# RWKV-7 recurrence and hardswish feed-forward on one core: r and a turned by VectorE, k and the state as half turns

## The chip, the cores and the metric

One core of a Trainium2 chip runs the whole program. The metric is the device time of one execution in microseconds, as the median of several runs. TensorE (PE) multiplies matrices and turns tiles by multiplying with an identity. VectorE (DVE), ScalarE (ACT) and GpSimd (POOL) do the elementwise work, and the DMA queues of SyncE (SP) and ScalarE issue the transfers. Each engine works through its own instructions in order.

## What is computed

```python
# r, k, v, w, a, b: (4, 8, 768, 40) f32
for t in range(S):
    y[:, :, t] = np.einsum('bhd,bhde->bhe', rt, state)
    Sa = np.einsum('bhde,bhe->bhd', state, at)
    state_decay = state * wt[:, :, None, :] - np.einsum('bhd,bhe->bhde', Sa, bt)
    state = state_decay + np.einsum('bhd,bhe->bhde', vt, kt)
x = y.transpose(0, 2, 1, 3).reshape(3072, 320)
h = x @ w_in                                   # (3072, 2048)
out = (h * np.clip(h + 3.0, 0.0, 6.0) / 6.0) @ w_out
```

## The kernel before

The sequence is cut into chunks of 64 steps. A **unit** is one chunk of two batch elements with all 8 heads; there are 24 units (NK), in groups of four (NU), and partitions hold 2 x 64 time steps. Inside a unit the recurrence becomes matrix products: decay products along the chunk (two scans on VectorE), scores between a, b, k, v and r, the inverse of a triangular matrix, and an update of the state.

Each unit has a part that doesn't need the state, **prepared ahead** (`prepare`), and its **own** part (`step`):

- `prepare`: W turns w and scans it (L549, L560 in gam); A and B turn a and b and multiply them by the decays (L593, L601); F multiplies a by b; K turns k (L474, L681); factor turns the decays and builds a tile of weighted k and b on GpSimd (L668); E multiplies k by a and masks the product (L521); EV multiplies E by v.
- `step`: RT and VT turn r and v (L484, copied out of PSUM by ScalarE at L839 and L872); S turns the state (L879, L884); R, C, U, UT, rS, H are products; y (L975) gives the output and the state's update together, which VectorE adds (L982, L987) and GpSimd scales (L983); move and move2 send the result to a tile `xt` by eight small DMAs on SP.

What has to be transposed is turned on TensorE in one of two forms. `turn_pairs` (and S, L879) turns four full 128x128 tiles into a bank tagged "one". `turn_halves` (L484) turns eight 64-row halves into a pair of banks. Before the change, w, k and the state go by the full form, and a, b, r, v by halves in later units (`halves`: from unit 4 in `step`, from unit 8 in `prepare`).

From about 200 us on, the order of work is written out by a loop over **blocks**, four to a unit (L1424). The stages of the own unit and of the unit prepared ahead for each block stand in OWN_STAGES and AHEAD_STAGES (L1338 to L1341); CLOSE_STAGES serves units 8 to 11, whose beginnings lie closer together. In a block, `together` (L1353) first lets TensorE do the block's products in the order PRODUCTS, then gives the other engines their work on the results in the order RESULTS. It counts PSUM banks (five at most), and the pairs of banks ("pair") are used in rotation, two of them. At FIRST_NARROW, if a feed-forward expansion is open, its 64-row matmuls are put in and its results follow (L1094 ScalarE, L1095 VectorE).

Between blocks, `feed` hands out pieces of feed-forward work: `expand` (h, L1079) into two banks and `contract` (o, L1120). An expansion can't begin until VectorE has read the one before (L1095). Every fourth unit VectorE also inverts four units' triangular matrices (L746, L752, some 60 small operations and three transposes of 128x1024 at L726, L755, L760), laid between the feed-forward pieces from block 2 of one unit to block 0 of the next but one. The products L781 and L804 ("third block") then follow in blocks 0 and 1 of two units.

Inputs are fetched one unit ahead by `fetch` on SP's queue: two DMAs for w, a, b and k, four for r and v.

## Time and profile before

Three runs took 794.69, 796.5 and 797.93 us; the median is 796.5. The profiled execution took 794.59 us with a span of 792.9 us.

| engine | busy us (share of span) | instructions |
|---|---|---|
| PE matmul | 727.6 (92%) | 14552 |
| PE weight load | 615.8 (78%) | 14552 |
| DVE | 496.8 (63%) | 986 |
| ACT | 307.1 (39%) | 648 |
| POOL | 161.5 (20%) | 296 |

The mean granted TensorE clock is 0.961 of full speed. A busy share is a mean over stages with different limits, so it is read by stretches. Of the time on TensorE, the two feed-forward products take most: h 251.2 us busy in 2304 matmuls and o 230.2 us in 768. Matmuls overlap in the pipeline, so what one costs TensorE is read from the chain of work in order of time (start, duration, what), where each piece ends when the next begins.

### The profile page before, as it was taken

To read this page: it belongs to the slowest core of one execution; us is meant where nothing else is said; L and a number is where in the kernel's file an instruction comes from. 1 tells how busy PE (TensorE), PEld (TensorE's weight loads), DVE (VectorE), ACT (ScalarE), POOL (GpSimd) and SP (SyncE) were. 2 spreads that over 40 slices of the span, in tenths; PEclk is the share of its full clock that TensorE was granted. 3 is DMA by queue.
4 is the path that set the end of the run, shared out by engine and by line. 5 is a ranking of instruction groups with operands and counts; after the bars stand their busy time and mean duration, and the time that the engine had idled before them with its cause. 6 is when DMAs were issued, how large, how long until landed. Compare 5 with 4: busy or idle time off the path is not lost.

```text
span 792.9 us, 32747 instructions
## 1 busy us (share of the span) xinstructions
PE 727.6 (92%) x14552; PEld 615.8 (78%) x14552; DVE 496.8 (63%) x986; ACT 307.1 (39%) x648; POOL 161.5 (20%) x296
## 2 busy tenths in 40 slices
PE   5735778999999999999999999999999999999997
PEld 4624667878778878888888888788888888888886
DVE  7898887689446699445898345888335982323210
ACT  2347663222553424443324453334443324412211
POOL 6403012421223203112303121303111201000000
PEclk9756898999999999999999999999999999999999
DMA  9683662420334321333323233223233101110100
GB/s 121 118 201 84 156 149 51 77 49 9 65 61 76 70 55 31 65 59 62 58 42 58 49 60 70 43 46 56 51 59 58 21 19 38 38 34 13 21 19 17
DMA packets 195004, 48.14 MB, mean 61 GB/s; under 512 B 178224, under 2 KB 193584, under 8 KB 194864
## 3 DMA queue, kind: packets, MB, share of 16 engines
q1 hardware_dynamic: 190560, 45.31, 30.9%
q8 instruction: 115, 1.88, 1.0%
q10 hardware_dynamic: 4304, 0.74, 0.7%
q14 instruction: 25, 0.20, 0.1%
HBM read 34.08 MB, written 3.93 MB: 48 GB/s over the span
## 4 chain that ended last, share of the span: by engine, by line
PE 76%; DVE 10%; issue 4%; DMA 3%; SPq 2%; ACT 2%; POOL 1%; DVEq 0%; POOLq 0%; ACTq 0%
PE h L1079 26%; PE o L1120 24%; PE pair L512 4%; PE pair L975 4%; PE one L474 2%; PE pair L484 2%; PE pair L893 2%; PE pair L861 2%; PE pair L695 1%; DVE wm L560 1%; DVE prods L549 1%; PE pair L929 1%; PE pair L913 1%; DVE prod L746 1%; DVE x L752 1%
## 5 line engine op out<-in xcount | busy, mean ns | idle before, releaser
L1079 PE MATMUL h<-xt,win 128*128 128x128 f32 (+1 forms) x2304 | 251.2, 283 | 4.9 <-DVE gt L1095 4.9
L1079 PEld LDWEIGHTS h<-xt,win 128*128 128x128 f32 (+1 forms) x2304 | 231.6, 193 | 23.0 <-issue 4.4
L1120 PE MATMUL o<-wout,gt 128*128 128x320 f32 x768 | 230.2, 443 | 0.0
L1120 PEld LDWEIGHTS o<-wout,gt 128*128 128x128 f32 x768 | 138.3, 190 | 50.7
L1094 ACT ACTIVATE gt<-h,three 128x512 f32<-128x512 f32 x96 | 63.1, 687 | 110.9 <-PE h L1079 110.5
L1095 DVE SCALAR_TENSOR_TENSOR gt<-gt,h 128x512 f32<-128x512 f32 x96 | 62.2, 683 | 67.2 <-ACT gt L1094 66.9
L746 DVE TENSOR_TENSOR prod<-x 128x30 f32<-128x30 f32 (+9 forms) x180 | 65.0, 361 | 9.0 <-POOL x L731 3.5
L525 DVE COPY_PREDICATED store<-mask,pair 128x512 f32<-128x512 int32 x40 | 29.0, 725 | 62.6 <-PE pair L512 62.5
L752 DVE TENSOR_TENSOR x<-x,prod 128x30 f32<-128x30 f32 (+9 forms) x180 | 64.4, 358 | 5.5
L668 POOL TENSOR_TENSOR KBt<-K,rgt 128x320 f32<-128x320 f32 x19 | 16.4, 865 | 204.5 <-ACT rgt L657 184.4
L983 POOL TENSOR_TENSOR yg<-ys,gam 128x512 f32<-128x512 f32 x20 | 25.5, 1273 | 147.5 <-DMA R<-in_r_dram 69.6
L982 DVE TENSOR_TENSOR ys<-pair,ys 128x512 f32<-128x512 f32 x20 | 13.8, 690 | 48.7 <-PE pair L975 43.5
L549 DVE TENSOR_TENSOR_SCAN prods<-wm,start 128x528 f32<-128x528 f32 x24 | 33.5, 1401 | 10.7 <-ACT wm L546 10.2
L839 ACT ACTIVATE RT<-pair 128x512 f32<-128x512 f32 x21 | 12.5, 597 | 59.1 <-PE pair L484 59.0
L975 PE MATMUL pair<-store,KBt 64*64 64x104 f32 x1280 | 33.1, 252 | 0.0
L560 DVE TENSOR_TENSOR_SCAN wm<-wm,start 128x528 f32<-128x528 f32 x24 | 31.1, 1297 | 0.8
L700 ACT ACTIVATE EV<-pair 64x320 f32<-64x320 f32 x44 | 18.9, 430 | 31.8 <-PE pair L695 30.4
L1138 ACT ACTIVATE ob<-o 128x320 f32<-128x320 f32 x22 | 9.6, 436 | 55.3 <-PE o L1120 34.6
L975 PEld LDWEIGHTS pair<-store,KBt 64*64 64x64 f32 x1280 | 29.1, 133 | 1.5
L814 ACT ACTIVATE tinv<-pair 32x256 f32<-32x256 f32 x48 | 18.0, 375 | 31.0 <-PE pair L804 30.4
L865 DVE TENSOR_TENSOR RR<-pair,EV 128x320 f32<-128x320 f32 x21 | 10.3, 489 | 23.7 <-PE pair L512 20.5
L897 ACT ACTIVATE store<-pair 128x320 f32<-128x320 f32 x24 | 10.5, 437 | 37.0 <-PE pair L913 33.6
(278 smaller groups left out, 1072.4 us busy)
## 6 DMA issues: line engine op xcount, KB each, us to landing
V<-in_v_dram SPq DMA_DIRECT2D x96, 40.0 KB
out_dram<-ob SPq DMA_DIRECT2D x47, 80.0 KB
R<-in_r_dram SPq DMA_DIRECT2D x92, 40.0 KB
B<-in_b_dram SPq DMA_DIRECT2D x42, 80.0 KB
store<-V SPq DMA_DIRECT2D x20, 160.0 KB
W<-in_w_dram SPq DMA_DIRECT2D x37, 80.0 KB
A<-in_a_dram SPq DMA_DIRECT2D x37, 80.0 KB
K<-in_k_dram SPq DMA_DIRECT2D x37, 80.0 KB
```

The costliest lines, as they stand in the source:

```text
L512: nc.tensor.matmul(out=o[i][half(q), n, :], lhsT=lhs[half(i, D), n ^ (2 * q * swap), half(q)], rhs=rhs[half(i, D), n ^ (2 * q * back), hal ...
L525: nc.vector.copy_predicated(out=x[:, :, 0:BL].rearrange("p (h i) t -> p i h t", i=2), mask=mask8, data=o[2])
L549: nc.vector.tensor_tensor_scan(out=prods[:].rearrange("p r m i -> p (r m i)"), data0=wm[:, 0:SCAN], data1=start[:], initial=0.0, op0=ALU.m ...
L560: nc.vector.tensor_tensor_scan(out=back, data0=back, data1=start[:], initial=0.0, op0=ALU.mult, op1=ALU.add)
L746: nc.vector.tensor_tensor(out=pv, in0=_ap(x[:], (i + 1) * L + i, [[L, n], [0, i]]), in1=_ap(x[:], i * L, [[0, n], [1, i]]), op=ALU.mult,)
L752: nc.vector.tensor_tensor(out=rest, in0=rest, in1=pv, op=ALU.add)
L975: nc.tensor.matmul(out=y[q][half(s), pr, :], lhsT=o[name][half(q), h * D:h * D + SLOT], rhs=m[name][half(q), x, :], start=(name == "K" and ...
L983: nc.gpsimd.tensor_tensor(out=yg[:], in0=m["ys"][:].rearrange("p r q t -> p r (q t)"), in1=o["G"][:], op=ALU.mult)
L1079: nc.tensor.matmul(out=hp[c][:, i, :], lhsT=lhsT, rhs=rhs, start=(begun[c] == 0), stop=(begun[c] == 3 * NQ - 1))
L1094: nc.scalar.activation(out=gt[:], in_=hp[c][:], func=AF.Relu, bias=three[:], scale=1.0)
L1095: nc.vector.scalar_tensor_tensor(out=gt[:], in0=gt[:], scalar=6.0, in1=hp[c][:], op0=ALU.min, op1=ALU.mult)
L1120: nc.tensor.matmul(out=op[:], lhsT=gts[c][:, n, :], rhs=wout[:, c * HJ + r * NQ + n, :], start=((split or r == 0) and c == 0 and n == 0), ...
```

## The change

Four things are changed together.

1. **r and a** of later units (r from unit 5, a from unit 8) are loaded by quarters of 32 partitions with two time steps on a partition side by side (`fetch_blocks`), and turned by VectorE's transpose of 32x32 blocks (`turn_blocks`). No TensorE turn, no PSUM and, for r, no ScalarE copy remain. The product of a with the decays, on VectorE before, is a GpSimd instruction on SBUF. A load of a is four DMAs in place of two, one of r eight in place of four; each brings 320 bytes to a run where it was 160.
2. **k and the state** are turned as eight half turns where they were four full ones (k from unit 8, the state from unit 4).
3. **Stages are moved.** K goes from block 2 to block 3, E from block 3 to block 0 of the next unit's time (AHEAD_STAGES). PRODUCTS is reordered, RT is no product any more (RT0 is the old form, for unit 4), and only W is left ahead of FIRST_NARROW.
4. **Smaller things.** The four larger moves into `xt` are issued by ScalarE's queue in place of SP's. The tiles of a and r grow from 512 to 672 columns, and the feed-forward tile `gt` has four buffers in place of five.

```diff
+    def blocked(name, i):
+        return i >= {"A": 2 * NU, "R": NU + 1}.get(name, NK)
+    def fetch_blocks(name, x, b, g, fresh):
+        t = homes[name]
+        for s in range(2):
+            for c in range(2):
+                rows = slice(s * SLOT + c * L, s * SLOT + c * L + L)
+                at = x.offset + (b * H + s) * T * D + g * BL * D
...
+                if fresh and c:
+                    nc.gpsimd.memset(t[rows, H * 2 * D:], 0.0)
+                first = (1 - c) * L
+                for k in range(2 if name == "R" else 1):
+                    n = 4 if name == "R" else 8
+                    y = bass.AP(tensor=x.tensor, offset=at + (s + k) * T * D if name == "R" else at,
+                                ap=[[2 * D, L], [(4 if name == "R" else 2) * T * D, n], [1, 2 * D]])
+                    nc.sync.dma_start(out=t[rows, first + k * H * D:first + k * H * D + n * 2 * D].rearrange(
+                        "p (n e) -> p n e", n=n), in_=y)
+        return t
+    def turn_blocks(to, t, name):
+        to = to[:].rearrange("p (j r) (q t c) -> p j q r c t", j=2, q=2, c=2)
+        x = t[:, L:L + 2 * H * D].rearrange("p (n c e) -> p n c e", c=2, e=D)[:, :, :, 0:L]
+        if name == "R":
+            x = x.rearrange("p (j q r) c e -> p j q r c e", j=2, q=2)
+            for j in range(2):
+                nc.vector.transpose(out=to[:, j], in_=x[:, j])
+            return
+        to = to.rearrange("p j q r c t -> p q (j r) c t")
+        nc.vector.transpose(out=to, in_=x.rearrange("p (q r) c e -> p q r c e", q=2))
@@ a_stage
+            if halves:
+                nc.vector.memset(_ap(o["wm"][:], 0, [[HB + 1, 2 * NB + 1]]), 0.0)
+                turn_blocks(at, o["AN"], "A")
+                nc.gpsimd.tensor_tensor(out=at[:], in0=at[:], in1=o["G"][:], op=ALU.mult)
@@ k_stage
-            x = turn_pairs(o["KN"])
+            x = turn_in(o["KN"], halves)
...
@@ s_RT
+            m["RT"] = turned("RT")
+            if blocked("R", i):
+                turn_blocks(m["RT"], o["RN"], "R")
+            else:
...
@@ s_S
-            sp = ps_any([P, 2, 2, P])
+            sp = ps_pair(4, SLOT) if halves else ps_any([P, 2, 2, P])
...
+                    if halves:
+                        for s in range(2):
+                            nc.tensor.transpose(out=sp[s][:, 2 * q + j, :], in_=x[half(s)],
+                                                identity=ident[half(s), half(s)])
@@ s_move
-                nc.sync.dma_start(out=dst, in_=src)
+                (nc.scalar if halves else nc.sync).dma_start(out=dst, in_=src)
@@ results
-                gt = ffn.tile([P, NQ, P], F32, name="gt", bufs=5)
+                gt = ffn.tile([P, NQ, P], F32, name="gt", bufs=4)
@@ the order
-    AHEAD_STAGES = [["W", "gam"], ["A", "B"], ["F", "K"], ["E", "factor"], [], [], [], ["EV"]]
+    AHEAD_STAGES = [["W", "gam"], ["A", "B"], ["F"], ["K", "factor"], ["E"], [], [], ["EV"]]
-    PRODUCTS = ["W", "S", "K", "RT", "VT", "A", "B", "factor",
-                "y", "EV", "R", "C", "U", "UT", "rS", "H", "E", "F"]
-    RESULTS = ["RT", "y", "W", "VT", "EV", "R", "S", "C", "A", "B", "move", "move2",
+    PRODUCTS = ["W", "S", "B", "K", "factor", "VT", "RT0", "E",
+                "y", "R", "C", "U", "UT", "rS", "H", "EV", "F"]
+    RESULTS = ["RT", "RT0", "y", "W", "VT", "EV", "R", "S", "C", "A", "B", "move", "move2",
                "U", "UT", "rS", "F", "K", "H", "E", "factor", "beside", "gam"]
-    TURNS = PRODUCTS[:3]
+    TURNS = ["W"]
...
+            first = [["RT" if blocked("R", i) else "RT0", "VT"]]
+            own[i, m] = step(i), first + OWN_STAGES[1:]
```

## The prediction

> **What bounds the kernel now.** I read the busy slices first (40 slices of 19.8 us), then busy time by stretches of 30 us, then the chain of waits in order of time, and last VectorE's and GpSimd's timelines inside one unit.
>
> ```profile
> PE   5735778999999999999999999999999999999997
> DVE  7898887689446699445898345888335982323210
> ...
> 440.00:470.00 30.00, 29.74 (x708) 25.56 (x701) 12.44 (x22) 15.82 (x38) 5.35 (x9) 1.00 0.34 61
> 470.00:500.00 30.00, 30.00 (x638) 25.63 (x637) 16.80 (x32) 11.57 (x27) 7.12 (x14) 1.00 0.34 59
> 500.00:530.00 30.00, 29.05 (x448) 24.60 (x448) 27.22 (x62) 9.24 (x21) 5.44 (x9) 1.00 0.27 48
> 710.00:740.00 30.00, 30.00 (x541) 25.87 (x540) 6.55 (x11) 7.70 (x15) 1.27 (x1) 1.00 0.15 32
> ```
>
> The columns of the stretches are length, then busy us of PE, PEld, DVE, ACT, POOL, then the granted clock, the DMA share and GB/s. From 200 us to the end PE is busy without a gap to speak of: 581.05 us of 593, where some 4 us are the wind-down behind the last matmul and 7.8 us are stalls. The granted clock there is 1.00, so no work is slowed by it. Whatever TensorE work is taken away after 200 us shortens the run, until another engine makes TensorE wait. The engine nearest to that is VectorE: 27.22 us of 30 in the stretch with an inversion (500 to 530), 12 to 17 in the others, and there alone PE loses nearly 1 us.
>
> **What TensorE loses.** Two pieces of the chain in order of time price the turns (start, us, what).
>
> ```profile
> 456.96 0.89 PE h L1079 x8
> 457.86 0.44 PE one L879 x4
> 458.29 1.09 PE h L1079 x16
> 459.38 0.49 PE pair L484 x16
> ```
>
> Four full turns of the state take 0.44 us, sixteen half turns 0.49, so eight take 0.245. Removed or shortened:
> - a, units 8 to 23: 16 x 0.245 = 3.9 us.
> - r, units 5 to 23: 19 x 0.245 = 4.65 us.
> - k, units 8 to 23, full to half: 16 x (0.44 - 0.245) = 3.1 us.
> - the state, units 4 to 23: 20 x 0.195 = 3.9 us.
>
> Together **15.6 us**, all behind 200 us; a steady unit loses 0.88 us of about 27. The switch from 128-row to 64-row matmuls (0.16 to 0.2 us: L484 x16 takes 0.65 directly behind o or full turns) stays once per block. Bank counts, worked out by `together`'s rule, stay within five in every steady block (5, 4, 4, 4 where it was 5, 5, 5, 4), so no block is split anew.
>
> **What the other engines gain, and what hides it.** The transposes come from this row, the GpSimd product from the next:
>
> ```profile
> L760 DVE STREAM_TRANSPOSE tt<-x 128x1024 f32<-128x1024 f32 x6 | 12.3, 2044 | 0.0
> ...
> L983 POOL TENSOR_TENSOR yg<-ys,gam 128x512 f32<-128x512 f32 x20 | 25.5, 1273 | 147.5 <-DMA R<-in_r_dram 69.6 <-DVE ys L982 63.2 <-DMA K<-in_k_dram 8.9
> ```
>
> 1024 columns take 2.04 us, so 512 about 1.05 (bounds: 0.68, the 128x512 product of L593, and 1.2, a little over half with a strided output). VectorE per unit: r +1.1 (two of 256 columns), a +0.4 (1.05 for 0.675), k and E only moved. ScalarE loses 0.6 (L839) and gains four DMA issues; GpSimd gains 1.27, with over 20 of each 30 us idle. The steady units' VectorE has 13 us of idle time in 30, so the sum of 1.5 us has room; what counts is whether it stands in front of something that TensorE awaits. Here is block 0 of unit 15, with an inversion running (VectorE, then the chain):
>
> ```profile
> 506.61 0.48 DVE L848 TENSOR_TENSOR state<-state,scale 128x320 f32<-128x320 f32 x1
> 508.50 0.69 DVE L982 TENSOR_TENSOR ys<-pair,ys 128x512 f32<-128x512 f32 x1 [1.40 <-PE pair L975]
> ...
> 513.95 1.29 DVE L1095 SCALAR_TENSOR_TENSOR gt<-gt,h 128x512 f32<-128x512 f32 x2
> ```
> ```profile
> 513.95 0.70 DVE gt L1095
> 514.65 0.14 issue
> 514.78 1.13 PE h L1079 x8
> ```
>
> Five terms follow.
> - **r's transposes** stand ahead of L848 and of y's additions. They fall into the 1.40 us in which VectorE waits for y; in plain units it waits 3.9. Cost 0 while r has landed (it is asked for a unit, some 27 us, ahead); without that cover, 1.1 us a unit.
> - **E's masking** (0.72, row L521) now stands in block 0 between the W scan and gam. So gt comes 0.72 later in the units whose VectorE has a queue, and the next expansion waits that much more: units 7, 11 and 15, 3 x 0.72 = 2.2 us.
> - **Plain units 10, 14, 18** (prepared ahead, without inversion or third block). y's products end at t = 0; VectorE does y and state (to 1.75), the scan (3.3), E (4.05), gam (6.2), gt (7.4), R and C (8.5), a's transpose (9.6); GpSimd the product of a (11.0). On PE, 3.06 us of feed-forward follow, then S and B, which need the banks that E's masking frees: 4.05 - 3.06 = 1.0 us of stall. Then F is due at 4.05 + 0.65 + 0.6 + 0.49 + 3.43 + 1.72 = 10.9, as a becomes ready. So 1.0 a unit, 3.0 us; bounds 0 (the banks prove free) and 1.5. Units 8, 9, 12, 13, 16 and 17 have a third block of 0.7 us and more feed-forward in between: about 0.
> - **GpSimd against VectorE**: VectorE's 128x30 product at 537.08 took 0.75 us while GpSimd's L668 ran from 536.93 to 537.79; the sum after it took 0.19.
>
> ```profile
> 536.93 0.86 POOL L668 TENSOR_TENSOR KBt<-B,rgt 128x320 f32<-128x320 f32 x1
> ```
> ```profile
> 537.08 0.75 DVE L746 TENSOR_TENSOR prod<-x 128x30 f32<-128x30 f32 x1
> ```
>
>   The new GpSimd product of 1.27 us can hold up one such operation in the inversions of units 11 and 15, and of some close units: 0 to 1.2 us each; I take 1.2 in all, since the inversion in the trace ends (tb at 540.07) 6.2 us before TensorE asks for it (546.32), and VectorE's net gain in that window is about 2.5 us.
> - **ScalarE's DMA issues**: 0.65 us each in the only stretch where ScalarE issues any (below), so 2.6 us in block 1 behind the copy of S, 0.9 each if the moves' issue on SP (3.50 for four) is the measure.
>
> ```profile
> 4.97 1.30 ACTq L458 DMA_DIRECT2D B<-in_b_dram  x2
> ```
>
>   In unit 12 ScalarE's S ends at 434.1 and its next work (L814) begins at 437.06: idle 2.97 against 2.6 to 3.5. In unit 13 the gap is 4.3, in unit 16 3.2, in unit 14 4.5. So 0 to 0.5 a unit, on half of 12 units; I take 0.6 in all, 4 at most. SP's queue gains 6 issues a unit and loses 4, 1.3 us net, with idle time of some 8 us a unit; the early chain at 247 to 256 us that runs over SP's issues may lengthen by as much: I take 0.6. Fewer gt buffers cost nothing: at most two expansions' tiles, four, are alive, since a contraction has nearly ended when the next results are written.
>
> Given back: 2.2 + 3.0 + 1.2 + 0.6 + 0.6 = 7.6 us. Net 15.6 - 7.6 = **8.0 us**. The profiled execution of 794.59 (span 792.9) would take 786.6. It is the fastest shown, 1.9 under the median of 796.5, so the median becomes **788.5 us**, and the likeliest case's own range 784 to 792.
>
> Two places of the Trainium skill bear on this. The rows at 537 us show VectorE held while GpSimd runs; "GPSIMD Engine Reference", Key points, says that the two share SBUF interfaces and collide on VectorE instructions with two SBUF inputs. By that every inversion operation behind the new product is exposed, 1.27 us in each of about five units, an estimate of 6 us where I take 1.2. The second: "DMA: Bandwidth & Descriptors", Issuing engines are not separate DMA queues, says issuing from a second engine saves only sequencer time, usually small. Here an issue takes 0.65 us, so the move relieves SP of 2.6 us a unit and loads ScalarE with it; by the rule that term would be zero.
>
> **Rivals.**
> - *The full gain.* All added work finds cover: 796.5 - 15.6 = 780.9. For it: VectorE idles 13 us of 30, ScalarE and GpSimd more. Against it: the stall at 514.65 exists already, and E is put ahead of it. Chance 0.15 (780 to 784).
> - *Given back.* The stalls reach 0.8 us a unit, close to the 0.88 saved: for instance 1.5 in the plain units, 1.2 for each inversion, 0.5 for ScalarE in each unit: 4.5 + 6 + 6 = 16, no net change, about 796. For it: four new hand-overs a unit (r on VectorE, a on GpSimd, E, moves). Against it: units 19 to 23 prepare nothing and keep 5 x 0.44 = 2.2. Chance 0.17 (792.5 to 800.5).
> - *VectorE becomes the bound in block 0, slower.* Its work there is y 1.7, scans and gam 3.6, L848 0.5 and gt 1.3; with r 1.1 and E 0.7 it is 8.9 us, while PE's block 0 without inversion takes some 6. If the following blocks don't absorb it, the added 1.8 is paid in all 12 units that prepare ahead (7 to 18), with the a transpose and product in front of F (1.05 - 0.675 + 1.27, about 1.65): 12 x 3.45 = 41 at most, 796.5 - 15.6 + 41 = 822; half of it 801. It decides from 1.3 us a unit on. Against it: block 2 leaves VectorE free for 5 us. Chance 0.15.
>
> **How the numbers follow.** The forecast (784 to 792.5) has 0.53. Faster by over 0.5%, about what this kernel's runs can tell from no change (below 792.5): 0.53 + 0.15 = 0.68. Within 0.5%: 0.17. Slower (over 800.5): 0.15. The range runs from the full gain, 780.5, to 797, the middle of the given-back case.
>
> **What would show it.** Right: PE's half turns of r and a gone, "one" left to w alone, VectorE busy up by some 27 us (19 x 1.1 + 16 x 0.4), PE's stalls after 200 us risen from 7.8 to about 15, at h behind gt and at S or B behind E. Wrong: transposes of 512 columns well over 1.2 us; PE waiting for VectorE's r, which would mean late loads; ScalarE's gt behind its DMA issues; F waiting for GpSimd in units other than 10, 14 and 18.

## The result, and the profile after

The change made the kernel slower. It takes 806.13 us (804.22 to 807.35) where the kernel before takes 795.6 in the same runs: a ratio of 1.0129, interval 1.0092 to 1.0167, some 10 us. The profiled execution took 804.22 us with a span of 802.5. TensorE's matmuls are busy 721.0 us where they were 727.6, VectorE 510.0 (496.8), ScalarE 298.5 (307.1), GpSimd 171.8 (161.5). So work was taken from TensorE, and the run got longer: the lost time is waiting.

The busy slices of the page after, and the granted clock beside them:

```profile
PE   5735778999979989999999999999999999999998
...
DVE  7898886688545599564799455899345983333110
...
PEclk9756978999989999999999999999999999999999
```

Two slices (20 us each) of PE that were 9 are lower, at 220 to 240 and at 280 to 300, and the first of them has a clock below full speed. Busy time by stretches (length, then PE, PEld, DVE, ACT, POOL, granted clock, DMA share, GB/s), with the dent's stretch in front:

```profile
230.00:260.00 30.00, 24.72 (x623) 20.34 (x616) 11.78 (x23) 13.03 (x32) 7.68 (x11) 0.89 0.40 76
440.00:470.00 30.00, 28.46 (x704) 23.48 (x691) 16.53 (x31) 13.82 (x33) 6.43 (x13) 1.00 0.35 65
470.00:500.00 30.00, 29.14 (x723) 24.44 (x722) 15.37 (x30) 11.65 (x26) 6.64 (x11) 1.00 0.39 78
500.00:530.00 30.00, 28.59 (x491) 24.52 (x484) 24.04 (x51) 9.98 (x22) 6.64 (x15) 1.00 0.35 66
710.00:740.00 30.00, 30.00 (x492) 25.03 (x494) 10.25 (x18) 7.43 (x13) 2.90 (x4) 1.00 0.13 28
```

The steady stretches from 440 to 530 lost 0.5 to 1.3 us more of PE's 30 to waiting than before, about what the removed turns were to save there (0.88 a unit). The stretch 230 to 260 lost 5.3, at a clock of 0.89. From 220 to 790 us PE is idle 7.7 us before and 22.5 after. What it waits for, in us, times and the longest one (200 to 790 us, after):

```profile
PE h L1144 <- DVE gt L1160: 5.9, 5, 2.3
PE pair L859 <- ACT F L692: 3.1, 1, 3.1
PE pair L836 <- DVE state L1052: 3.0, 4, 1.0
PE pair L682 <- issue: 2.8, 4, 1.1
PE pair L859 <- DVE wm L640: 1.3, 4, 0.5
```

Before, h's wait for gt was 2.8 us, and the second and third of these lines did not exist:

```profile
PE h L1079 <- DVE gt L1095: 2.8, 3, 1.0
```

To place the loss I read from the timeline when each unit's y products end (L975 before, L1040 after); the difference of two of them is a unit's length. Sums in us, of the profiled executions of five kernels (kone, ra_s_act and late are explained below). One execution each stands behind the columns, and ahead of unit 5 executions differ by more than most of these sums: unit 4's products end at 220.4 to 222.5 us in before, split_before, stall2 and stall5, which do the same work up to there.

| units | before | after | kone | ra_s_act | late |
|---|---|---|---|---|---|
| 5 | 23.66 | 30.66 | 26.38 | 25.02 | 23.64 |
| 6 | 27.37 | 28.01 | 29.63 | 29.97 | 27.38 |
| 7 | 38.27 | 39.99 | 39.70 | 40.78 | 38.28 |
| 8 | 25.45 | 26.60 | 25.77 | 25.22 | 27.54 |
| 9 to 18 | 289.68 | 288.51 | 286.27 | 281.87 | 281.76 |
| 19 to 23 | 124.45 | 123.93 | 123.96 | 124.00 | 123.96 |
| 5 to 23 | 528.88 | 537.70 | 531.71 | 526.86 | 522.56 |

Units 5 to 8 lose 10.5 us, 7.0 of them in unit 5; units 9 to 18 gain 1.2 in place of 8.8 (10 x 0.88), and units 19 to 23 gain 0.5 in place of 2.2.

**Unit 5.** TensorE in the kernel after (start, us, what, and the wait before it):

```profile
230.52 1.34 PE L1185 MATMUL o<-wout,gt 128*128 128x320 f32 x4
232.21 0.46 PE L534 MATMUL pair<-ident,K 64*128 64x64 f32 x8 [0.34 <-ACT S L947]
232.51 0.41 PE L702 MATMUL pair<-ident,rgam 64*128 64x64 f32 x8
232.85 0.69 PE L682 MATMUL pair<-bt,at 40*64 40x64 f32 x32
236.69 1.08 PE L859 MATMUL pair<-zs,tt 32*32 32x32 f32 x64 [3.15 <-ACT F L692]
237.70 4.42 PE L1185 MATMUL o<-wout,gt 128*128 128x320 f32 x8
```

and in the kernel before:

```profile
230.03 0.66 PE L474 MATMUL one<-ident,K 128*128 128x128 f32 x4
230.62 0.46 PE L648 MATMUL pair<-ident,rgam 64*128 64x64 f32 x8
231.01 0.69 PE L628 MATMUL pair<-bt,at 40*64 40x64 f32 x32
231.64 0.75 PE L804 MATMUL pair<-zs,tt 32*32 32x32 f32 x64
232.32 2.42 PE L1120 MATMUL o<-wout,gt 128*128 128x320 f32 x8
```

Before, k lay in "one", factor and F shared a pair, and the third block took the other: L648, L628 and L804 followed each other without a gap. After, k's half turns share a pair with factor and F takes the other of the two pairs, so the third block (L859) must wait for a pair; what ends the wait in the trace is the last of ScalarE's copies of F. ScalarE in the same stretch after (ACTq is its queue's DMA issues):

```profile
231.56 0.60 ACT L947 ACTIVATE S<-pair 128x512 f32<-128x512 f32 x1
232.21 2.32 ACTq L1088 DMA_DIRECT2D xt<-yg  x3
234.57 0.37 ACT L689 ACTIVATE F<-pair 32x256 f32<-32x256 f32 x1 [2.41 <-DMA xt<-yg]
234.96 0.64 ACT L692 ACTIVATE F<-pair 32x256 f32<-32x256 f32 x2
235.61 0.37 ACT L689 ACTIVATE F<-pair 32x256 f32<-32x256 f32 x1
235.99 0.65 ACT L692 ACTIVATE F<-pair 32x256 f32<-32x256 f32 x2
```

Three moves are issued in 2.32 us in front of F's copies, which end at 236.64; L859 begins at 236.69. And there is a second price: the same eight contraction matmuls take 4.42 us behind this wait and 2.42 before the change. The granted clock explains it:

```profile
235.00:240.00 5.00, 3.31 (x69) 2.46 (x70) 0.00 (x0) 3.55 (x10) 1.67 (x2) 0.50 0.35 61
290.00:295.00 5.00, 5.00 (x104) 4.64 (x104) 4.62 (x14) 0.60 (x1) 0.00 (x0) 0.70 0.07 16
```

It falls to one half from 234.9 to 241.8 us, and from 289.6 to 293.0 behind a wait of 2.29 us for gt. The missing clock adds up to 5.1 us; 0.9 of it lies inside the first wait, so the matmuls lost some 4.3 us. Before, the clock is 1.00 from 200 to 790 us, and no wait there is longer than 1.21 us.

So the books are: 14.8 us more waiting (22.5 - 7.7) and 4.3 us of clock, against 8.8 us that units 5 to 23 got longer; the remainder, about 10.3 us, is the work of TensorE that went, of 15.6 forecast.

### The profile page after: what moved, and what is told of

The parts are those of the page before. It is cut to its first block, busy times and chain, and to the rows that moved or that the text cites. A ratio compares the mean times of both kernels' runs of the same rounds, so it can differ in the third digit from the quotient of the medians.

```text
span 802.5 us, 32704 instructions
## 1 busy us (share of the span) xinstructions
PE 721.0 (90%) x14416; PEld 604.6 (75%) x14416; DVE 510.0 (64%) x1024; ACT 298.5 (37%) x629; POOL 171.8 (21%) x316
## 3 DMA queue, kind: packets, MB, share of 16 engines
HBM read 39.81 MB, written 3.93 MB: 55 GB/s over the span
## 4 chain that ended last, share of the span: by engine, by line
PE 55%; DVE 21%; issue 9%; DMA 5%; SPq 4%; ACT 3%; POOL 2%; ACTq 1%; POOLq 0%; DVEq 0%
PE h L1144 20%; PE o L1185 17%; PE pair L562 3%; DVE prod L801 3%; DVE x L807 3%; SPq L464 3%; PE pair L1040 3%; DVE prods L599 2%; DVE gt L1160 2%; DVE wm L610 2%; PE pair L958 1%; DMA W<-in_w_dram 1%; PE pair L534 1%; ACTq L1088 1%; PE pair L978 1%
## 5 line engine op out<-in xcount | busy, mean ns | idle before, releaser
L1185 PE MATMUL o<-wout,gt 128*128 128x320 f32 x768 | 233.7, 448 | 0.0
L1185 PEld LDWEIGHTS o<-wout,gt 128*128 128x128 f32 x768 | 140.3, 193 | 52.0 <-issue 2.4
L807 DVE TENSOR_TENSOR x<-x,prod 128x30 f32<-128x30 f32 (+9 forms) x180 | 66.5, 370 | 5.5
L736 DVE TENSOR_TENSOR kt<-pair,rgam 128x512 f32<-128x512 f32 x19 | 13.1, 687 | 48.8 <-PE pair L702 48.4
L642 POOL TENSOR_TENSOR at<-at,gam 128x512 f32<-128x512 f32 x16 | 20.4, 1272 | 81.3 <-DVE at L478 77.4
L1040 PE MATMUL pair<-store,KBt 64*64 64x104 f32 x1280 | 32.6, 250 | 0.5 <-DVE bt L655 0.5
L1040 PEld LDWEIGHTS pair<-store,KBt 64*64 64x64 f32 x1280 | 29.2, 133 | 1.1 <-DVE bt L655 0.6
L947 ACT ACTIVATE S<-pair 128x512 f32<-128x512 f32 x20 | 11.9, 597 | 37.9 <-PE pair L534 22.2
```

Of the source, the lines that this page charges most:

```text
L807: nc.vector.tensor_tensor(out=rest, in0=rest, in1=pv, op=ALU.add)
L1040: nc.tensor.matmul(out=y[q][half(s), pr, :], lhsT=o[name][half(q), h * D:h * D + SLOT], rhs=m[name][half(q), x, :], start=(name == "K" and ...
L1185: nc.tensor.matmul(out=op[:], lhsT=gts[c][:, n, :], rhs=wout[:, c * HJ + r * NQ + n, :], start=((split or r == 0) and c == 0 and n == 0), ...
```

## Experiments

Each ratio is against the kernel before, run beside it (793 to 796 us). None leaves out any work. All that are built on the change, r_only too, keep its four gt buffers. Their loads of r and a also bring each byte twice (HBM read, by the pages: 34.08 MB before, 39.81 after), which no run separates from their larger number.

| kernel | what differs | us | ratio, interval |
|---|---|---|---|
| after | the change | 806.13 | 1.0129, 1.0092 to 1.0167 |
| moves_sp | after, moves on SP | 808.04 | 1.018, 1.0124 to 1.0236 |
| early | moves_sp, E and a earlier on VectorE | 797.82 | 1.0057, 1.0034 to 1.008 |
| early_act | after, E and a earlier on VectorE | 801.51 | 1.0093, 1.0061 to 1.0125 |
| kone | after, k as full turns in "one" | 797.74 | 1.0041, 1.0019 to 1.0062 |
| kone_early | kone, E and a earlier on VectorE | 798.6 | 1.0066, 1.0042 to 1.009 |
| r_only | before, r by VectorE | 792.5 | 0.9987, 0.997 to 1.0004 |
| r_act | r_only, moves on ScalarE | 797.09 | 1.0044, 1.0029 to 1.006 |
| ra_old | before, r and a by VectorE | 798.06 | 1.0053, 1.0033 to 1.0073 |
| ra_old_act | ra_old, moves on ScalarE | 795.56 | 0.9992, 0.9967 to 1.0017 |
| ra_s_act | ra_old_act, state as half turns | 791.9 | 0.998, 0.9965 to 0.9995 |
| ra_s_early | ra_s_act, a earlier on VectorE | 793.86 | 1.0004, 0.9992 to 1.0016 |
| prod_new | ra_s_act, PRODUCTS as in kone | 796.23 | 1.002, 1.0002 to 1.0037 |
| ahead_new | ra_s_act, AHEAD_STAGES as after | 805.3 | 1.0128, 1.011 to 1.0146 |
| split_before | before, r's and a's loads cut in two | 796.91 | 1.0036, 1.0021 to 1.0051 |
| late | ra_s_act, new forms from unit 9 on | 791.1 | 0.995, 0.9932 to 0.9969 |
| late_sp | late, moves on SP | 794.87 | 1.0003, 0.9988 to 1.0017 |
| stall2 | before, two more additions | 795.94 | 1.0033, 1.0018 to 1.0049 |
| stall5 | before, five more additions | 808.32 | 1.0199, 1.0161 to 1.0237 |

### First: ScalarE's issues, VectorE's order, or r and a themselves

**moves_sp** puts the four moves back on SP.

```diff
-                (nc.scalar if halves else nc.sync).dma_start(out=dst, in_=src)
+                nc.sync.dma_start(out=dst, in_=src)
```

> The changed kernel with one edit: the four larger moves into xt go back to SP's queue. Theory 1 (ScalarE held by the moves' issues: in unit 5, from 230.8 to 234.5 us, four issues stand in front of the copies of F, TensorE waits 3.15 us for them, and the granted clock falls to 0.89 in that stretch): 797 to 799 us, interval of unit 5 back from 30.7 to about 24 us. Theory 2 (SP's queue, longer by the quarter loads of r and a, delays the early units): no better than 806, perhaps 808, since SP gets 2.6 us a unit more. Theory 3 (VectorE's order, E masked ahead of gam): 806, within 2.

It was no faster (808.04). Unit 5 still took 29.81 us, with a wait of 2.19 us at L859 and the clock at 0.50 behind it, so ScalarE's issues lengthen that wait but do not make it. TensorE now also waited 5.5 us for the moves (h for xt), in units 8, 12 and 16: with the new loads and the moves both on SP's queue, the moves come late. The theory that ScalarE's issues alone are the loss fell.

**early** adds to it another order of VectorE's results: E's masking in front of W's scan, a's transpose in front of R's addition.

```diff
-    RESULTS = ["RT", "RT0", "y", "W", "VT", "EV", "R", "S", "C", "A", "B", "move", "move2",
-               "U", "UT", "rS", "F", "K", "H", "E", "factor", "beside", "gam"]
+    RESULTS = ["RT", "RT0", "y", "E", "W", "VT", "EV", "A", "R", "S", "C", "B", "move", "move2",
+               "U", "UT", "rS", "F", "K", "H", "factor", "beside", "gam"]
```

> The moves on SP as in moves_sp, and in RESULTS E's masking ahead of the W scan and a's transpose ahead of R's addition. Theory 3: TensorE's waits at S and B, at the third block and at F shrink by some 0.5 us in each of 12 units, so 5 to 6 us below moves_sp. Theory 1 or 2: within 1.5 of moves_sp.

797.82, ten us under moves_sp, and of the waits for xt one of 0.4 us is left. But unit 5's wait (2.19 us) and both falls of the clock are still there. VectorE's order is worth something; it isn't what unit 5 loses.

**ra_old** has r and a by VectorE only: k and the state as full turns, stages in the old order, moves on SP.

```diff
-            x = turn_in(o["KN"], halves)
+            x = turn_in(o["KN"], False)
...
-            sp = ps_pair(4, SLOT) if halves else ps_any([P, 2, 2, P])
+            sp = ps_any([P, 2, 2, P])
...
-    AHEAD_STAGES = [["W", "gam"], ["A", "B"], ["F"], ["K", "factor"], ["E"], [], [], ["EV"]]
+    AHEAD_STAGES = [["W", "gam"], ["A", "B"], ["F", "K"], ["E", "factor"], [], [], [], ["EV"]]
```

> Only r and a by VectorE; k and the state stay full turns, the stages stay where they were, the moves stay on SP; gt keeps four buffers. TensorE's work falls by 8.55 us. If nothing waits: 787 to 788 beside a before of 796. Theory 2 (quarter loads late or in SP's way): 796 or more. If F waits for GpSimd's product of a in each unit: 791 to 795.

798.06, slower than before. L859's wait on F is gone, and TensorE waits for transfers (us, times, longest):

```profile
PE h L1144 <- DMA xt<-yg: 6.5, 6, 2.2
...
PE pair L534 <- DMA B<-in_b_dram: 1.8, 2, 1.4
```

The fetch of b for a unit prepared ahead was issued at 242.7 us where it was issued at 236.1 before, and TensorE's last wait for it ended at 245.9. SP's queue, with six more issues a unit, is late.

**r_only** is ra_old with a in the old form too.

```diff
-        return i >= {"A": 2 * NU, "R": NU + 1}.get(name, NK)
+        return i >= {"R": NU + 1}.get(name, NK)
```

> Only r by VectorE, all else as before but for four gt buffers. TensorE's work falls by 4.65 us: 791 to 792 if VectorE's two transposes are covered as the prediction had it. Theory 2: 796 or more, since r's eight loads are the larger part of SP's new issues. If r's transposes hold up VectorE: 796 to 800.

792.5, a ratio not told from 1. In its profile units 5 to 8 take 118.18 us (114.75 before), units 9 to 18 285.30 (289.68): the gain exists, and units 5 to 8 give most of it back.

### Second: k's half turns, and SP's queue by itself

**kone** is the change with k as four full turns in "one", where it is put in front of S.

```diff
-            x = turn_in(o["KN"], halves)
+            x = turn_in(o["KN"], False)
...
-    PRODUCTS = ["W", "S", "B", "K", "factor", "VT", "RT0", "E",
+    PRODUCTS = ["W", "K", "S", "B", "factor", "VT", "RT0", "E",
...
-    TURNS = ["W"]
+    TURNS = ["W", "K"]
```

> The changed kernel with k turned by full turns into the bank tagged one (4 in place of 8 half turns, TensorE's work 3.1 us more). Theory 4 (k's half turns and the decay's turns share a pair of banks, F has the other, so in unit 5 the third block's second product, which takes the next pair, waits until ScalarE has copied F and the decays; 2.2 us in moves_sp, 3.15 in the changed kernel, and 2.2 us more because the clock falls): unit 5's interval falls from 30.7 to about 26, and the time from 806 to 802 in spite of the 3.1 us. Rival (the banks are not what it waits for): 806 + 3 = 809.

797.74: seven us better than after (1.0041 against 1.0129), though by the prediction's price it does 3.1 us more work on TensorE. Its unit 5:

```profile
231.31 0.60 PE L524 MATMUL one<-ident,K 128*128 128x128 f32 x4
231.91 0.46 PE L702 MATMUL pair<-ident,rgam 64*128 64x64 f32 x8
232.31 0.69 PE L682 MATMUL pair<-bt,at 40*64 40x64 f32 x32
232.93 0.75 PE L859 MATMUL pair<-zs,tt 32*32 32x32 f32 x64
233.61 2.42 PE L1185 MATMUL o<-wout,gt 128*128 128x320 f32 x8
```

The third block follows F at once again, o takes its 2.42 us, and the clock doesn't fall behind 200 us. With ScalarE's moves as in after, this shows that k's place in a pair made the 3.15 us wait (k is also put in front of S, but unit 5's wait is missing in every run with k in "one", in whichever order). In units 9 to 18 the half turns of k also lose, 2.24 us (288.51 against 286.27) where they should save 1.95.

**early_act** is early with the moves on ScalarE, as in after.

> As early (E masked ahead of the W scan, a's transpose ahead of R's addition), but with the moves on ScalarE's queue as in the changed kernel. If the changed kernel's waits on VectorE's order cost what early against moves_sp showed (10 us, of which the waits for xt in units 11, 15 and 16 are about 6): 802. If early's gain came from the waits for xt alone: 806. If ScalarE's issues cost in the early units: worse than early's 798 in unit 5 by 1 us, and 0.3 elsewhere.

801.51: between after and early. With this order of VectorE's results SP looks like the better queue for the moves (1.0057 against 1.0093), with the order of after ScalarE (1.0129 against 1.018), but in both cases the intervals overlap, so neither is shown.

**split_before** is the kernel before with the loads of r and a cut into eight and four DMAs over the same bytes.

```diff
                 for s in range(2):
-                    engine.dma_start(out=t[rows, 4 * s:4 * s + 4, 0:D],
-                                     in_=y[s::2].rearrange("h t e -> t h e"))
+                    for c in range(2 if name == "R" and i > NU else 1):
+                        m = L if name == "R" and i > NU else BL
+                        engine.dma_start(out=t[q * BL + c * m:q * BL + c * m + m, 4 * s:4 * s + 4, 0:D],
+                                         in_=y[s::2, c * m:c * m + m].rearrange("h t e -> t h e"))
```

(and the same with two parts for a.)

> The kernel before with nothing but more issues on SP: each load of r from unit 5 and of a from unit 8 is cut into two DMAs of 32 partitions with the same bytes in all, so 8 for r and 4 for a, as in the change. Theory 2 (SP's issues, 0.65 us each, 3.9 us a unit more, make b and xt late): 799 to 803, with TensorE waiting for the DMA of b in unit 5 and for xt in units 11 and 15, as in ra_old. Rival (SP has room, the loss of ra_old is VectorE's and GpSimd's): within 1.5 us of before.

796.91, ratio 1.0036: between theory and rival. Six more issues a unit on SP cost 2.9 us even where nothing else is changed. In its profile unit 8 shows 1.3 of it (26.72 against 25.45); the others are within 0.4 of before.

**ra_old_act** is ra_old with the moves on ScalarE.

> As ra_old (r and a by VectorE, k and state full, stages where they were), but with the four larger moves on ScalarE's queue, so SP has 4 issues fewer a unit. Theory 2: the waits for xt (6.5 us) and b (1.8 us and a dip of the clock) go, so 798 - 8 = 790. Rival (the waits for xt only hide VectorE's): 796 or more.

795.56: the waits for xt are gone, and 4.8 us come back (0.9992 against 1.0053), of the 8 expected; a wait of 1.69 us for b in unit 6 is still there.

### Third: the state's half turns, without the moved stages

**ra_s_act** is ra_old_act with the state as half turns: the change without k's half turns and without the moved stages.

> The changed kernel with k as full turns and with AHEAD_STAGES and PRODUCTS in the order of before: r and a by VectorE, the state as half turns, the moves on ScalarE. Against ra_old_act (1.0 above before) it has only the state's half turns added, 3.9 us less on TensorE. If what cost 3.7 us from ra_old_act to kone was the moved stages: 792 (-2 to -4 against before). If it was the state's half turns: as kone, +3.

791.9, ratio 0.998: the first version that is faster than before beyond its interval, by 0.2%. Units 9 to 18 take 281.87 us, 7.81 less than before. Three terms of the prediction give 10 x (0.245 + 0.245 + 0.195) = 6.85 for a, r and the state, so there the gain is all paid out in sum (r_only alone gained 4.4 of it, where r's price gives 2.45). Units 5 to 8 lose 6.2, part of it behind a wait of 1.78 us for gt that the clock follows down to 0.50 from 286 to 293 us.

**ra_s_early** adds a's transpose in front of R's addition.

```diff
-    RESULTS = ["RT", "RT0", "y", "W", "VT", "EV", "R", "S", "C", "A", "B", "move", "move2",
+    RESULTS = ["RT", "RT0", "y", "W", "VT", "EV", "A", "R", "S", "C", "B", "move", "move2",
```

> As ra_s_act, with a's transpose ahead of R's addition in RESULTS, so that GpSimd's product of a is ready 1.1 us sooner. If F's wait for that product costs what the prediction took (0.3 to 1 us in plain units): 1 to 3 us below ra_s_act. If F seldom waits for it, but R's addition and C's masking, now later, hold up the third block: 0 to 2 us above.

793.86, if anything 2 us slower. In ra_s_act F begins 0.11 us behind GpSimd's product of a in units 10 and 14, without a gap on TensorE, and 1.9 us and more behind it elsewhere, so it gains nothing by an earlier one.

**r_act** is r_only with the moves on ScalarE.

> Only r by VectorE, all else as before, and the four larger moves on ScalarE, so SP's issues stay at their old number (4 more for r, 4 fewer moves). If SP's issues took part of r_only's 4.65 us: 790 to 791 beside a before of 794.5. If VectorE's transposes took it: as r_only, -1.

797.09, 4.5 us slower than r_only (1.0044 against 0.9987), so with r alone the moves are better left on SP. Where the time goes the two profiles don't say: units 5 to 23 take 527.18 against 526.96 us (with a fall of the clock worth 1.7 us behind a wait of 1.9 for gt, which r_only has without a fall), the end 0.8 more, and 4.0 us lie ahead of the end of unit 4's products, where the two kernels do the same work.

**kone_early** is kone with the order of VectorE's results of early.

> As kone, with E's masking ahead of the W scan and a's transpose ahead of R's addition. If the moved E, masked behind the scan, is what the new order costs (early_act stood 3.6 us nearer to before than the changed kernel): kone's +3.1 becomes -0.5 or better. If the new order costs by its bank pairs, not by E's place on VectorE: +2 to +4.

798.6, no better than kone. So E's place among VectorE's results is not what the new order costs. In its profile one wait of 1.59 us at 495 us (for which the trace names no releaser) and the clock's fall behind it make unit 14 3.3 us longer; another fall stands at 289 us.

### Fourth: where the gain lies, and which moved stage costs

**late** is ra_s_act with the new forms begun later: r, the state and the moves from unit 9, a from unit 14. Those of the units before stay in the old form.

```diff
-        return i >= {"A": 2 * NU, "R": NU + 1}.get(name, NK)
+        return i >= {"A": 14, "R": 9}.get(name, NK)
...
-            sp = ps_pair(4, SLOT) if halves else ps_any([P, 2, 2, P])
+            late = i >= 9
+            sp = ps_pair(4, SLOT) if late else ps_any([P, 2, 2, P])
...
-                (nc.scalar if halves else nc.sync).dma_start(out=dst, in_=src)
+                (nc.scalar if i >= 9 else nc.sync).dma_start(out=dst, in_=src)
...
-    PRODUCTS = ["W", "K", "S", "RT0", "VT", "B", "factor", "y", "EV", "R", "C", "U", "UT", "rS", "H", "E", "F"]
+    PRODUCTS = ["W", "S0", "K", "S", "RT0", "VT", "A0", "B", "factor", "y", "EV", "R", "C", "U", "UT", "rS", "H", "E", "F"]
```

(S0 and A0 are the old forms of S and A in the earlier units.)

> The kernel of ra_s_act (r and a by VectorE, state as half turns, k full, stages in the old order, moves on ScalarE), with the new forms begun later: r, the state and the moves from unit 9, a from unit 14; before that the old forms. Theory 6 (the gain is real in units 9 to 18, where ra_s_act took 281.87 us against 289.68 before, and is lost in units 5 to 8, where it took 121.2 against 114.75): units 5 to 8 as before (114 to 116), units 9 to 18 as in ra_s_act (281 to 283), in all 785.5 to 788, no granted clock of 0.50. Rival (the first units with the new forms pay some 6 us wherever they stand, because their first loads and banks fall out of step): units 9 to 12 longer by that, in all 791 to 794.

791.1, ratio 0.995: faster than both kernels, 0.5% under before, 1.8% under after. Units 5 to 7 are as before to 0.02 us and units 9 to 18 as in ra_s_act (281.76), so the loss of units 5 to 7 belongs to the new forms in those units. The rival holds for a part: unit 8, next to the start, lost 2.1 us. The median stayed 3 us above the expected range, of which this explains two. In the profile units 5 to 23 gained 6.3 us, and 2.5 of them are lost again ahead of unit 5 (unit 4's products end at 224.36 against 221.84), where TensorE's work is that of before. Its first stretch, with the clock at 1.00:

```profile
220.00:250.00 30.00, 29.93 (x723) 23.96 (x721) 17.42 (x34) 13.45 (x34) 9.22 (x15) 1.00 0.41 72
```

**late_sp** has the moves on SP throughout.

> late with the four larger moves on SP in every unit. Theory 6 (SP's queue is the limit only where units follow each other at 24 us; but r and a together put six more issues of about 0.7 us a unit on it, and ra_old showed TensorE waiting 6.5 us for xt): 1 to 4 us above late. Rival (the waits for xt come from the early units alone): the same as late within 0.7.

794.87, all the gain gone. TensorE waits for the moves again, once for 3.0 us, and behind that the clock falls:

```profile
PE h L1151 <- DMA xt<-yg: 6.3, 5, 3.0
```

**ahead_new** is ra_s_act with K moved to block 3 and E to block 0, as in the change.

```diff
-    AHEAD_STAGES = [["W", "gam"], ["A", "B"], ["F", "K"], ["E", "factor"], [], [], [], ["EV"]]
+    AHEAD_STAGES = [["W", "gam"], ["A", "B"], ["F"], ["K", "factor"], ["E"], [], [], ["EV"]]
```

> ra_s_act with the changed AHEAD_STAGES (K in block 3, E in block 0), the order of products kept. Theory 7 (E's masking in block 0 holds the banks that the plain units await, as the prediction's second term says, 0.8 us in each of units 10 and 14 and 0.5 in unit 18, and some 0.4 in the others): 3 to 4.5 us above ra_s_act, 795 to 796.5. Rival (the order of PRODUCTS costs it): within 1 us of ra_s_act.

805.3: 11.8 us slower than ra_s_act (1.0128 against 0.998), three times what I expected. Units 10 and 14 take 29.5 us where they took 27.89, units 11 and 15 37.9 where they took 35.2, and the clock falls three times (once in ra_s_act). Its waits, and the wait in unit 10 with VectorE's work ahead of it:

```profile
PE h L1144 <- DVE gt L1160: 6.3, 4, 2.0
PE pair L940 <- DVE state L906: 3.6, 3, 1.2
...
369.04 1.53 DVE L599 TENSOR_TENSOR_SCAN prods<-wm,start 128x528 f32<-128x528 f32 x1
370.50 0.74 DVE L475 STREAM_TRANSPOSE RT<-R 128x256 f32<-128x256 f32 x2
371.17 0.68 DVE L906 TENSOR_TENSOR state<-state,scale 128x320 f32<-128x320 f32 x1
...
372.00 0.47 PE L940 MATMUL pair<-ident,state 64*128 64x64 f32 x8 [1.19 <-DVE state L906]
```

S's turn waits for the decay of the state (L906), which here stands behind W's scan and r's transposes on VectorE. In ra_s_act and in after r's transposes come ahead of y's additions and the scan. The reason is the rule of five banks: with E in block 0 and the old order of products, W, VT and y take five and E two more, so `together` splits block 0 of units 8 to 19, and r's transposes and the decay go with the second part. In the new order E shares a pair with VT, and no such block is split. So ahead_new does not price the moved stages; it shows what a split block costs.

**prod_new** has the products in kone's order, and AHEAD_STAGES as before.

```diff
-    PRODUCTS = ["W", "K", "S", "RT0", "VT", "B", "factor", "y", "EV", "R", "C", "U", "UT", "rS", "H", "E", "F"]
+    PRODUCTS = ["W", "K", "S", "B", "factor", "VT", "RT0", "E",
+                "y", "R", "C", "U", "UT", "rS", "H", "EV", "F"]
```

> ra_s_act with the changed order of PRODUCTS (k's full turn added in front), AHEAD_STAGES as before the change. Theory 7: within 1 us of ra_s_act, 791 to 793. Rival (the order of PRODUCTS costs it): 3 to 4.5 us above ra_s_act.

796.23, ratio 1.002 against 0.998, some 3 us slower, of which its profile has 0.9 in units 5 to 8 and 0.9 in units 19 to 23. So the order of products costs by itself, and theory 7's "within 1 us" fails. kone differs from prod_new in AHEAD_STAGES alone, with no block split: units 9 to 18 take 286.27 against 282.04 us, so there the moved stages cost 4.2 us in the profiles, about what theory 7 expected. The ratios (1.0041 and 1.002) point the same way, but their intervals overlap.

### Fifth: does a wait of TensorE bring the clock down

**stall2** and **stall5** are the kernel before, with y's addition on VectorE done two or five more times in units 12 to 14 and 16 to 18.

```diff
+            for _ in range(5 if 12 <= i < 19 and i != 15 else 0):
+                nc.vector.tensor_tensor(out=by_banks(yg), in0=y[2][:, :, :, 0:BL], in1=x, op=ALU.add)
             nc.vector.tensor_tensor(out=x, in0=y[2][:, :, :, 0:BL], in1=x, op=ALU.add)
```

> The kernel before, with y's addition on VectorE done twice more (into yg, which GpSimd overwrites) in units 12, 13, 14, 16, 17 and 18: 2 x 0.69 = 1.4 us later state and gt, no other change, same result. Theory 8 (a wait of TensorE below about 1.3 us costs only itself): waits of 0 to 1.4 us in six units, 0 to 8 us in all, no granted clock of 0.50. Rival (the clock falls after any wait): over 10 us, 0.50 in most of the six units.

> The same with five more additions, 3.45 us later state and gt in the six units. Theory 8 (a wait of about 2 us or more is followed by a granted clock of 0.50 over 3.4 to 7.3 us, so it costs 1.7 to 3.6 us on top of itself; five of the seven waits of 2.2 us and more in the profiles so far were): waits of 2 to 3.4 us in six units, 12 to 20 us of waiting, and 0.50 behind most of them, another 8 to 20 us: 20 to 40 us in all. Rival (the dips in the changed kernel have another cause than its waits): the waiting alone, 12 to 20 us, and no 0.50.

stall2 took 795.94 (ratio 1.0033), stall5 808.32 (1.0199). stall5's waits between 440 and 640 us, and the granted clock around the two longest:

```profile
PE h L1081 <- DVE gt L1097: 4.6, 1, 4.6
PE pair L804 <- DVE wm L590: 3.4, 2, 2.2
PE pair L861 <- DVE state L989: 2.7, 2, 1.3
```

```profile
455.00:462.00 7.00, 5.46 (x118) 4.89 (x116) 6.73 (x13) 1.70 (x4) 3.31 (x5) 1.00 0.48 94
462.00:467.00 5.00, 4.37 (x83) 4.33 (x84) 2.36 (x5) 2.21 (x6) 0.00 (x0) 0.66 0.11 27
...
521.00:528.00 7.00, 5.28 (x40) 4.98 (x42) 6.53 (x18) 0.60 (x1) 0.71 (x3) 0.52 0.01 2
528.00:535.00 7.00, 7.00 (x122) 6.01 (x118) 5.65 (x14) 1.38 (x2) 0.00 (x0) 1.00 0.22 47
```

Half speed follows the wait of 2.2 us and sets in within that of 4.6, in a kernel that otherwise never shows it behind 200 us: the wait brings the fall. The rival's "no 0.50" is refuted. The sizes were mine to get wrong: fewer waits came about than I meant, 12.5 us in this stretch where the kernel before has 2.4, and the clock took (5 x 0.34) + (7 x 0.48) = 5.1 us, 0.7 of it inside a wait. 10.1 + 4.4 = 14.5, close to the 14.2 by which units 5 to 23 got longer, so a fall costs 1.7 to 2.7 us on top of its wait. In stall2 one wait of 2.39 us was followed by none:

```profile
517.00:524.00 7.00, 6.83 (x131) 6.56 (x132) 6.62 (x18) 1.28 (x2) 0.00 (x0) 1.00 0.22 46
```

So the length of a wait alone doesn't decide, and theory 8's bound of about 2 us is not one.

## Why the prediction was wrong, point by point

The forecast was 8 us faster, and the kernel is 10 us slower. The ratios give the main steps back: 1.0129 after, 1.0041 with k in "one" (kone, 7 us), 0.998 with the stages and products in their old order too (ra_s_act, 5 us), 0.995 with the new forms begun behind the early units (late, 2 us).

**The work removed** (15.6 us) was about right where the new forms run undisturbed: 7.8 us in units 9 to 18 of ra_s_act and late, where the prediction's prices for r, a and the state give 6.85. It was wrong for k, whose half turns cost seven us in all (kone against after). In the last five units 0.5 came of 2.2. With the moves on SP it is 1.5 (122.92 us in early and moves_sp against 123.95 after), and behind unit 23 the run is 0.8 us shorter, so ScalarE's issues take about half of the 2.2.

**"Bank counts stay within five in every steady block, so no block is split anew"** is the step that failed. The count is not the only limit: pairs rotate, and there are two of them. k in "one" kept a pair free for the third block; k in a pair took it. In unit 5 the next pair then hung on ScalarE's copies of F, with three moves' issues in front of them: 3.15 us of wait, and 7.0 us of the unit with the clock's fall. I reckoned banks for the steady blocks and not for units 4 to 8, where a third block stands beside a preparation. The count itself was right: no steady block was split.

**The early units** were the place. Apart from unit 7's share of E's masking, the prediction gave them 0.6 us ("the early chain"). Units 5 to 8 lost 10.5 in the change, 6.2 in ra_s_act, 2.1 in late, where the new forms begin behind them. The stretches that the prediction shows begin at 440 us; in the kernel before PE already loses 1.9 of 30 us from 260 to 290, with VectorE busy for 22.3, so "there alone PE loses" was not so.

**"r's transposes: cost 0."** In units 9 to 18 this held. In the early units it did not: at the beginning of unit 5 the products of the third block (L836) wait 1.0 us for the state's addition, which stands behind r's transposes, and the wait for gt in unit 7 is 1.9 us in r_only where it was 0.9. (L836's waits in units 8, 13 and 17, 0.5 to 0.9 us, are in after and kone but not in ra_s_act or prod_new: they come with the moved stages.)

**"k and E only moved."** E's masking in front of gt was given 2.2 us in units 7, 11 and 15. h's waits for gt rose from 2.8 to 5.9, but ra_s_act, with E in its old place, has 4.1, and prod_new, with E in its old place and the new order of products, 5.0 where kone has 5.4. So E's place is worth some 0.4 of it, and that term was too large. The plain units were given 1.0 each; kone lost 0.81, 0.80 and 0.47 in units 10, 14 and 18 against ra_s_act, and the wait is there as forecast, R for the banks that E's masking frees, but 0.42 us long. That term was right in mechanism, and not far off in size. What was left out is the rest of the moved stages: kone takes 4.4 us more in units 9 to 18 than ra_s_act, and these three units explain 2.1.

**Durations.** The transposes were cheaper than taken (1.1 and 1.05 us). The groups of the kernel after:

```profile
L642 POOL TENSOR_TENSOR at<-at,gam 128x512 f32<-128x512 f32 x16 | 20.4, 1272 | 81.3 <-DVE at L478 77.4 <-PE pair L534 1.9 <-DVE wm L640 1.9
...
L475 DVE STREAM_TRANSPOSE RT<-R 128x256 f32<-128x256 f32 x38 | 14.3, 415 | 0.0
...
L478 DVE STREAM_TRANSPOSE at<-A 128x512 f32<-128x512 f32 x16 | 11.1, 692 | 0.0
```

0.69 us for 512 columns, and two of 256 in 0.76 us as the timeline has them (461.20 to 461.96). VectorE's busy time rose by 13 us, not 27. The GpSimd product takes 1.27 us as forecast, and the 1.2 us for its collision with VectorE did not show: units 11 and 15 gained 0.74 us each in ra_s_act, where the prices give 0.69.

**Queues.** ScalarE's issues and SP's were given 0.6 us each, 4 at most. They are worth 4 to 5 us either way. SP with r's and a's loads and the moves makes TensorE wait 5.5 to 6.5 us for xt (moves_sp, ra_old, late_sp); ScalarE with the moves loses 4.5 us where only r's loads are new (r_act against r_only). By the Trainium skill, "DMA: Bandwidth & Descriptors", Issuing engines are not separate DMA queues, a second issuing engine saves only sequencer time, usually small relative to the DMA itself. Here that time is 0.72 us for a move, and the choice of the queue moves the run by 0.5 to 0.6%.

**The clock.** The prediction wrote that the granted clock is 1.00 and no work is slowed by it, and did not ask what a new wait does to it. Some 4.3 of the 10 us lost are that.

**The rivals.** The slower one, VectorE as the bound in block 0, forecast 801 to 822: the measured 806 lies in it. Its mechanism is a part at most: gt's waits rose by 3.1 us, and its place was to be units 7 to 18, while most of the loss lies in unit 5 with PE waiting for ScalarE. So its time was right by luck, and its cause mostly not.

Not tried: k's half turns in the old order of stages (by the kernel's own count the block that holds F and K would need six banks and be split), late with the moves back on SP in the last five units, and five gt buffers with the new forms.

## What to carry to other kernels

A tile moved from a buffer of its own into a rotation of two takes the place of whoever comes next, so count not how many banks a block holds, but who frees the one that the next product will get, and what stands in front of that on its engine. Judge a change at the densest units of the schedule, not at the steady ones: where the time between units is shortest, every added instruction on a queue becomes a wait; begin the new form behind them if it pays only later. In a kernel like this one, whose matrix engine is never idle, price a wait of 2 us at 2 to 5, since the clock may fall behind it. And when one part of a change is put back alone, check by the schedule's own rules that nothing else moves with it: ahead_new split a block.

## What the runs showed of the hardware that I had not expected

The granted clock of TensorE falls to 0.50 at waits of 1.35 to 4.6 us (ra_old's was the shortest, stall5's the longest) in a run that is else busy without a gap, and stays there for 3.41 or 6.83 us. No fall stands behind waits of 1.3 us and less; of those between 1.3 and 2.4 us some have one and others not (1.78 us in ra_s_act has, 1.78 in kone has not; 2.17 in stall5 has, 2.39 in stall2 has not).

The records of the clock show what a wait's length leaves out. Each level lasts 3.41 us or a multiple of it, so a trace can be cut into windows of 3.41 us at whose edges alone the clock changes. Between 200 and 775 us of the twenty traces, 13 windows at full clock hold 1.89 us or more without a matmul, and 0.50 follows each; of 16 windows with 1.45 to 1.86 us it follows ten; of some 3300 with less, none. stall2's 2.39 us were cut by an edge, with 1.44 us on the larger side, and ra_old's wait of 2.20, which no fall follows either, with 1.19. What decides in the windows between, these runs don't show. The Trainium skill, "TensorE: Matmul & The Clock Gate", Part 1, says that the clock is halved after an idle window of about 3.4 us, and that the windows run free. The two levels, the lengths of the falls and the part that the windows' edges play agree with it; but a window need not be idle as a whole here: 1.9 us of 3.41 were always enough, and 1.45 us sometimes.

Where the four moves are issued by ScalarE, they hold its queue for 2.96 to 3.04 us in most units (3.71 in unit 5), with a median of 0.72 us each, so a DMA issue there costs more than a copy of 128x512 (0.60 us).
